# Loading wq in two pieces and wo's row blocks 26 to 29 in one, in a cached attention decode kernel with a gated feed-forward branch

## The chip, the cores and the metric

The kernel runs on one core of one Trainium2 chip. The core has a matrix engine (TensorE, PE in the profile, with PEld for its weight loads), a vector engine (VectorE, DVE), an activation engine (ScalarE, ACT), GpSimd (POOL) and SyncE (SP), which here only issues transfers. Sixteen DMA engines move data between HBM and the on-chip memory of 128 partitions. The metric is the device time in microseconds (us) of one execution. What the profiler sees of an execution, from its first to its last instruction, is called the span.

## What is computed

One token passes through an attention block with a long cache and through a feed-forward block, and a scalar gate mixes the two:

```python
g = sigmoid((x * gate_w).sum(-1))             # x: 512 numbers
q = (x @ wq).reshape(32 heads, 128)            # wq: 512 x 4096
scores = q . k_cache * 128 ** -0.5             # 8 groups of 4 heads, 32768 positions
o = softmax(scores) . v_cache                  # k_cache, v_cache: 8 x 32768 x 128
a = o.reshape(4096) @ wo                       # wo: 4096 x 512
b = (silu(x @ w_gate) * (x @ w_up)) @ w_down   # 512 x 1792, 512 x 1792, 1792 x 512
out = g * a + (1 - g) * b
```

All inputs are bf16. The two caches are 67 MB each; wq and wo are 4.2 MB each and the three feed-forward matrices 1.8 MB each. Everything is read once, 148 MB in all.

## The kernel before

**Memory.** One tensor, `page`, holds three pages of 64 KB in each of the 128 partitions. A K or V group (8.4 MB) fills one page. K groups go by turns into pages 0 and 1, V groups into page 2. Until V0 comes, page 2 holds wq (32 KB per partition) and the gate and up matrices behind it. After the last K group, page 0 takes `w_down` and wo.

**Transfers.** SP issues all loads on one queue, in an order that is written out by hand (lines 349 to 387): wq, x and `gate_w` (one row of 1 KB each), gate, up, K0 in two halves, K1, and then by turns a K group and a V group, each behind a wait for the page to be free. K1 needs no wait. V0 waits until TensorE has finished with gate and up (`sem_pe_h`), since they share page 2 with wq. K2 waits for the 32 transposes of K0 (`sem_tr`), V1 for the last matmul on V0 (`sem_v_done`). The last V group comes in four pieces, and then wo comes in the pieces of `WO_CUTS` (line 59), each with a semaphore of its own. wo is seen as 32 row blocks: every partition holds 32 rows of 512 numbers, and a block is one such row on all partitions, 1 KB each.

**The head.** TensorE transposes x and `gate_w` (L383), VectorE writes the columns into a zero-padded tile and multiplies them for the gate, and TensorE waits for wq (`sem_q`, line 393) before the q projection and then the gate and up projections (L400, 64 matmuls). VectorE turns q into blocks (`qblk`, L637) and computes the feed-forward activations.

**The groups.** For every K group VectorE transposes 32 units of the page into two slots (L707), and TensorE multiplies each with q (L445) into the scores. VectorE takes the maximum (L716), GpSimd reduces it over partitions (L308), ScalarE takes the exponentials (L567) and rearranges them (L580), and TensorE multiplies them with the V group (L472). TensorE goes through the groups in a loop in which V of one group comes ahead of the scores of the next.

**The tail.** TensorE multiplies the attention output with wo. Row blocks 0 to 19 are taken by `emit_wide` as rows of 512 columns (L517). The blocks behind them go through `emit_wo` and `emit_rows` (lines 236 to 258, L239), four matmuls of 128 columns per block, which wait for the semaphore of each piece. The pieces from index `KL` = 4 on are taken at lines 764 and 765, outside of the main block, so the branch out of that block (L267) lies in front of them. Then VectorE copies the row to bf16 (L768), and SP and ScalarE's queue store half of it each (L262).

Of the kernel before, what the change touches and what calls it, by code (L numbers as in the profile page):

```python
# [14 lines left out]
def bass_gated_mix__gqa_block_cached__swiglu_ffn__decode_kernel(  # L15
# [23 lines left out]
    KC = D // 128  # L39
# [16 lines left out]
    assert S % 128 == 0 and NT == 256 and G == 8 and RB * NS * 4 == 4096  # L56
    assert KC * H * DH + 2 * KC * F <= PAGE and (FC + WOJ) * NOUT <= PAGE

    WO_CUTS = [0, 16, 20, 24, 26, 28, 30, 32]
    KW = 2  # L60
    KL = 4
    WIDE = WO_CUTS[KW]
    RQ = 4
# [13 lines left out]
    assert RQ * HPG <= 32 and RQ * DH == 512 and FC % 2 == 0  # L77
    assert WO_CUTS[-1] == WOJ and FC % 2 == 0

# [7 lines left out]
    with ExitStack() as es:  # L87
        def S_(name):
            return es.enter_context(nc.semaphore(name))

        sem_q = S_("s_q")
# [9 lines left out]
        sem_ld_wd = S_("s_ld_wd")  # L101
        sem_wo = [S_(f"s_wo{i}") for i in range(len(WO_CUTS) - 1)]
        sem_tr = S_("s_tr")
# [99 lines left out]
        wq_v = page[:, w0 : w0 + KC * H * DH].rearrange("p (c n) -> p c n", c=KC)  # L203
# [29 lines left out]
        def rows(p, a, b):  # L233
            return page[:, p * PAGE + a * DH : p * PAGE + b * DH]

        def emit_rows(pe, lhs, rhs, last):
            for oc in range(OC):
                e = oc % RPS
                ins = pe.matmul(  # L239
                    ps_c[32 * oc : 32 * oc + (1 if e else SW), 0:128],  # L240
                    lhs(e),
                    rhs[:, oc * 128 : (oc + 1) * 128],
                    start=False,
                    stop=last,
                    skip_group_check=True,
                )
            return ins

        def emit_wo(pe, k):
            pe.wait_ge(sem_wo[k], 16)  # L250
            for j in range(WO_CUTS[k], WO_CUTS[k + 1]):
                ins = emit_rows(
# [14 lines left out]
        with nc.Block("main") as block:  # L267
# [49 lines left out]
            @block.sync  # L317
            def _(sp):
                def cache(src, j, p, a=0, b=NT):
                    return sp.dma_start(  # L320
                        rows(p, a, b),
                        src[0, j, :, :].rearrange("(p r) d -> p r d", r=NT)[:, a:b, :].rearrange(
                            "p r d -> p (r d)"
                        ),
                    )

                def load_k(j):
                    if j >= K_PAGES:
                        sp.wait_ge(sem_tr, UNITS * (j - K_PAGES + 2))
                    p = j % K_PAGES  # L330
                    late = {0: sem_k0, G - 1: sem_k7}.get(j)
                    if late is None:
                        cache(A_k_cache, j, p).then_inc(sem_k[p], 16)
                    else:
                        cache(A_k_cache, j, p, 0, NT // KH).then_inc(sem_k[p], 16)
                        cache(A_k_cache, j, p, NT // KH, NT).then_inc(late, 16)

                def load_v(j):
                    if j:
                        sp.wait_ge(sem_v_done, VTURN * (j + 1))  # L340
                    else:
                        sp.wait_ge(sem_pe_h, KC)
                    if j < G - 2:
                        cache(A_v_cache, j, V_PAGE).then_inc(sem_v, 16)
                    else:
                        cache(A_v_cache, j, V_PAGE, 0, V6_CUT).then_inc(sem_v, 16)
                        cache(A_v_cache, j, V_PAGE, V6_CUT, NT).then_inc(sem_v6, 16)

                sp.dma_start(wq_v, A_wq.rearrange("(p c) n -> p c n", c=KC)).then_inc(sem_q, 16)
                sp.dma_start(x2[0:1, :], A_x[0, :, :]).then_inc(sem_ld_x, 16)  # L350
                sp.dma_start(x2[1:2, :], gate_w.unsqueeze(0)).then_inc(sem_ld_x, 16)
                for w, (src, sem) in enumerate(((B_w_gate, sem_fg), (B_w_up, sem_fu))):
                    sp.dma_start(
                        wgu[:, w, :, :], src.rearrange("(p c) f -> p c f", c=KC)
                    ).then_inc(sem, 16)
                load_k(0)
                for j in range(G - 1):
                    load_k(j + 1)
                    load_v(j)
                sp.wait_ge(sem_tr, UNITS * G)  # L360
                sp.dma_start(wd_v, B_w_down.rearrange("(p j) n -> p j n", j=FC)).then_inc(
                    sem_ld_wd, 16
                )
                def load_wo(k):
                    a, b = WO_CUTS[k], WO_CUTS[k + 1]
                    src = A_wo.rearrange("(p j) n -> p j n", j=WOJ)
                    sp.dma_start(wo_v[:, a:b, :], src[:, a:b, :]).then_inc(sem_wo[k], 16)  # L367

                for k, sem in enumerate(sem_v7):
                    a, b = V7_CUTS[k], V7_CUTS[k + 1]  # L370
                    sp.wait_ge(sem_v_done, VTURN * (G - 1) + b // (RQ * VB))
                    cache(A_v_cache, G - 1, V_PAGE, a, b).then_inc(sem, 16)
                for k in range(len(sem_wo)):
                    load_wo(k)

            @block.tensor
            def _(pe):
                def emit_q():
                    pe.wait_ge(sem_eye, 1)
                    pe.wait_ge(sem_ld_x, 32)  # L380
                    x2v = x2.rearrange("o (p c) -> o c p", c=KC)
                    for c in range(KC):
                        ins = pe.matmul(  # L383
                            ps_m[:, M_X0 + 2 * c : M_X0 + 2 * c + 2],
                            x2v[:, c, :],
                            eye2[:, :],
                            start=True,
                            stop=True,
                        )
                    ins.then_inc(sem_pe_x, 1)  # L390
                    pe.wait_ge(sem_dve_prod, 1)
                    pe.wait_ge(sem_xz, 2)
                    pe.wait_ge(sem_q, 16)
                    pe.wait_ge(sem_psw, 1)

                    def strips(c, base, n, width, at, ps):
                        x = [pe.compute_val(c * XW + (96 - 32 * s)) for s in range(NSTRIP)]
                        w = [pe.compute_val(c * n + (base + at(i))) for i in range(2 * NSTRIP)]
                        for i in range(2 * NSTRIP):
                            ins = pe.matmul(  # L400
                                ps_sc[:, ps(i) * 512 : ps(i) * 512 + width],
                                slot[:, bass.ds(x[i % NSTRIP], 128)],
                                page[:, bass.ds(w[i], width)],
                                start=False,
                                stop=False,
                                skip_group_check=True,
                            )
                        return ins

                    with pe.Fori(0, KC, 1) as c:  # L410
                        strips(
                            c, w0, H * DH, 512, lambda i: (2 * (i % 4) + i // 4) * 512, lambda i: i // 4
                        ).then_inc(sem_pe_q, 1)
                    pe.wait_ge(sem_fg, 16)
                    pe.wait_ge(sem_fu, 16)
                    with pe.Fori(0, KC, 1) as c:
                        strips(
                            c, w1, F, FS, lambda i: (i // 4) * KC * F + (i % 4) * FS, lambda i: 2 + i // 4
                        ).then_inc(sem_pe_h, 1)
                    pe.wait_ge(sem_const, 4)  # L420
                    pe.wait_ge(sem_dve_qT, 1)
                    qc0 = q_blk.rearrange("p (n l) -> p n l", l=QP)[:, :, 0]
                    for s in range(NSTRIP):
                        ins = pe.matmul(
                            ps_m[:, M_P0 + s * 32 : M_P0 + (s + 1) * 32],
                            spread[:, s, :],
                            qc0,
                            start=True,
                            stop=True,
                        )  # L430
                    ins.then_inc(sem_pe_qp, 1)
# [75 lines left out]
                def emit_wide():  # L507
# [5 lines left out]
                    for k in range(KW):  # L513
                        pe.wait_ge(sem_wo[k], 16)
                        for j in range(WO_CUTS[k], WO_CUTS[k + 1]):
                            c = j % NSTRIP
# [13 lines left out]
                    for k in range(KW + 1, KL):  # L530
                        emit_wo(pe, k)

                emit_q()
                with hinted(pe, "groups", 1, G + 4) as (p, arm):
                    with pe.If(p < G + 3):
# [227 lines left out]
        pe, dve = nc.tensor, nc.vector  # L763
# [37 lines left out]
```

## Time and profile before

| what | us |
|---|---|
| median of three runs | 349.87 (349.70 to 349.89) |
| the profiled execution | 349.6 |
| its span | 348.2 |
| VectorE busy | 191.2 |
| TensorE matmuls busy | 182.1 |
| ScalarE busy | 92.8 |
| wq, from its issue to its landing | 12.4 |
| wo's first piece (2 MB), from issue to landing | 24.9 |
| wo's four pieces of 256 KB, median from issue to landing | 26.8 |

The page gives the busy time of each engine over the span; the forty slices show when it lies. Time from issue to landing counts the waiting behind earlier transfers of the same queue, so that a late landing need not be a slow transfer. The DMA view of a stretch gives the packets that began in it and the time they took as a share of sixteen engines; from the two the mean time of one packet can be worked out. A packet carries the row of one partition. In a short stretch the share can be over 100%, because a packet counts where it begins.

### The profile page before, as it was taken

The numbers are of one execution on the slowest core, as the hardware profiler recorded it, in microseconds if no ns is written. First come the engines' busy times: TensorE is split into PE (matmuls) and PEld (weight loads), VectorE is DVE, ScalarE is ACT, GpSimd is POOL, SyncE is SP. The second block draws the span as 40 slices with busy tenths as digits, with TensorE's granted clock in tenths as the row PEclk, the third lists the DMA queues.
The fourth block names the chain that finished last, engine by engine and source line by source line (L and its number), as shares of the span: only waits on it lengthen the run. The fifth ranks groups of instructions, "written<-read, shape, count | busy, mean of one in ns | idle before, by whom it ended". The sixth has DMA issues, their size and how long they took to land.

```text
span 348.2 us, 7729 instructions
## 1 busy us (share of the span) xinstructions
PE 182.1 (52%) x2755; PEld 111.1 (32%) x2755; DVE 191.2 (55%) x311; ACT 92.8 (27%) x220; POOL 8.3 (2%) x29
## 2 busy tenths in 40 slices
PE   0393553555425570565435560556445485667555
PEld 0141442443124420443124420443134334432112
DVE  4024996996059911995069802994079829940001
ACT  1002001901730039002630057003630066037000
POOL 4000000000000000000000000000000000000000
PEclk9999555555855556555855576555655576559856
DMA  8999989989899898998989989899898999999996
GB/s 324 419 459 425 482 384 459 474 369 482 376 467 474 369 482 369 474 474 369 482 369 474 474 369 482 369 474 474 369 482 369 440 448 429 422 413 430 429 427 261
DMA packets 4766, 148.14 MB, mean 425 GB/s; under 512 B 538, under 2 KB 540, under 8 KB 1308
## 3 DMA queue, kind: packets, MB, share of 16 engines
q1 hardware_dynamic: 4760, 148.12, 98.9%
q8 instruction: 1, 0.02, 0.0%
q14 instruction: 1, 0.01, 0.0%
q10 hardware_dynamic: 4, 0.00, 0.0%
HBM read 148.11 MB, written 0.00 MB: 425 GB/s over the span
## 4 chain that ended last, share of the span: by engine, by line
DMA 49%; PE 21%; DVE 18%; issue 9%; SPq 2%; DVEq 1%; ACT 0%
DMA page<-in_A_k_cache_dram 39%; DVE slot L707 17%; PE ps_sc L445 9%; DMA page<-in_A_wo_dram 7%; PE ps_o L472 7%; PE ps_sc L400 4%; DMA E<-in_gate_w_dram 3%; SPq L367 2%; DVE qblk L637 0%; SPq L320 0%; DVE E L654 0%; DVE oT L695 0%; DVEq L703 0%; DVE E L663 0%; PE ps_o L486 0%
## 5 line engine op out<-in xcount | busy, mean ns | idle before, releaser
L707 DVE STREAM_TRANSPOSE slot<-page 128x512 f32<-128x512 f32 x256 | 167.0, 690 | 92.9 <-DMA page<-in_A_k_cache_dram 80.9
L445 PE MATMUL ps_sc<-qcur,slot 128*128 128x16 bf16 x2048 | 103.8, 179 | 119.7 <-DVE slot L707 106.4
L445 PEld LDWEIGHTS ps_sc<-qcur,slot 128*128 128x128 bf16 x2048 | 81.2, 107 | 143.3 <-issue 142.2
L472 PE MATMUL ps_o<-page,ET 128*16 128x512 bf16 x512 | 47.5, 546 | 19.7 <-issue 15.2
L580 ACT ACTIVATE ET<-E 32x256 bf16<-32x256 bf16 x128 | 52.8, 412 | 1.4
L562 ACT ACTIVATE nbias<-gmax 128x4 f32<-128x4 f32 x8 | 1.6, 206 | 179.1 <-POOL gmax L308 179.1
L472 PEld LDWEIGHTS ps_o<-page,ET 128*16 128x16 bf16 x512 | 16.0, 117 | 47.6 <-issue 37.9
L567 ACT ACTIVATE E<-ps_sc,nbias 128x256 bf16 x32 | 21.8, 851 | 1.8 <-ACT nbias L562 1.8
L400 PE MATMUL ps_sc<-page,slot 128*128 x64 | 14.8, 391 | 1.0 <-DVE prod_col L618 1.0
L716 DVE TENSOR_REDUCE pmax<-ps_sc 128x4 f32<-128x1024 f32 x8 | 9.8, 1225 | 4.7 <-PE ps_sc L445 4.7
L739 DVE TENSOR_REDUCE oT<-ps_o 128x4 f32<-128x64 f32 x1 | 0.2, 224 | 21.3 <-PE ps_o L486 21.3
L562 ACT ACT_TABLE_LOAD x8 | 10.3, 1283 | 0.1
L576 ACT ACTIVATE acc<-ps_o 128x512 f32<-128x512 f32 x8 | 4.8, 606 | 20.4 <-PE ps_o L472 20.4
L308 POOL PARTITION_ALL_REDUCE gmax<-pmax x8 | 3.0, 371 | 292.1 <-DVE pmax L716 292.1
L400 PEld LDWEIGHTS ps_sc<-page,slot 128*128 x64 | 6.6, 103 | 8.9 <-issue 3.8
L567 ACT ACTIVATION_READ_ACCUMULATOR E<-ps_sc,nbias x32 | 9.3, 290 | 0.0
L486 PE MATMUL ps_o<-ident_f,acc 128*128 128x128 f32 x32 | 5.7, 305 | 5.6 <-ACT acc L576 4.9
L383 PE MATMUL ps_m<-eye,E 2*128 2x2 bf16 x4 | 0.3, 166 | 13.2 <-DMA E<-in_gate_w_dram 13.2
L486 PEld LDWEIGHTS ps_o<-ident_f,acc 128*128 128x128 f32 x32 | 3.6, 150 | 10.0 <-ACT acc L576 8.4
L498 PE MATMUL ps_w<-page,vec 128*1 x14 | 5.3, 376 | 2.2 <-issue 0.8
L627 DVE CAST E<-ps_sc 128x1024 bf16<-128x1024 f32 x1 | 1.2, 1225 | 8.8 <-PE ps_sc L400 8.8
L614 DVE CAST xT<-ps_m 128x4 bf16<-128x4 f32 x1 | 0.2, 163 | 8.3 <-PE ps_m L383 8.3
(63 smaller groups left out, 34.6 us busy)
## 6 DMA issues: line engine op xcount, KB each, us to landing
page<-in_A_k_cache_dram SPq DMA_DIRECT2D x4, 4096.0 KB, 36.9
page<-in_A_v_cache_dram SPq DMA_DIRECT2D x2, 4096.0 KB, 22.4
page<-in_A_wq_dram SPq DMA_DIRECT2D x1, 4096.0 KB, 12.4
page<-in_A_v_cache_dram SPq DMA_DIRECT2D x2, 2048.0 KB, 14.0
page<-in_A_v_cache_dram SPq DMA_DIRECT2D x1, 3072.0 KB, 14.3
page<-in_A_wo_dram SPq DMA_DIRECT2D x1, 2048.0 KB, 24.9
page<-in_B_w_gate_dram SPq DMA_DIRECT2D x1, 1792.0 KB, 15.6
page<-in_B_w_up_dram SPq DMA_DIRECT2D x1, 1792.0 KB, 19.5
```

The source lines that it names most:

```text
L367: sp.dma_start(wo_v[:, a:b, :], src[:, a:b, :]).then_inc(sem_wo[k], 16)
L400: ins = pe.matmul(ps_sc[:, ps(i) * 512 : ps(i) * 512 + width], slot[:, bass.ds(x[i % NSTRIP], 128)], page[:, bass.ds(w[i], width)], start= ...
L445: ins = pe.matmul(ps_sc[:, bass.ds(c0 + u * (SLOTS * RPU * NS) + (s * RPU + r) * NS, NS),], sv[:, s, r, e // 2, e % 2, :], qcur[:, e, :], ...
L472: ins = pe.matmul(ps_o[32 * c : 32 * c + VW, :], ET[:, k * VW : (k + 1) * VW], rows(V_PAGE, n, n + RQ), start=(k < NSTRIP), stop=(k >= NT ...
L486: ins = pe.transpose(ps_o[:, q * 128 : (q + 1) * 128], acc[:, q * 128 : (q + 1) * 128], ident_f[:, :],)
L498: pe.matmul(ps_w[0:1, :], vec[:, bass.ds(n, 1)], page[:, bass.ds(n * NOUT + o0, NOUT)], start=False, stop=False, skip_group_check=True,)
L562: act.activation(nbias[:, :], gmax[:, :], ACT.Copy, scale=-SCALE).then_inc(sem_nbias, 1)
L567: act.activation(ev[:, h, :, :], scv[:, h, :, :], ACT.Exp, bias=nbias[:, h : h + 1], scale=SCALE, accum_out=esum[:, bass.ds(j * HPG + h, 1 ...
L576: act.activation(acc[:, :], ps_o[:, :], ACT.Copy).then_inc(sem_acc, 1)
L580: ins = act.activation(etv[QP * i : QP * (i + 1), :, g, :], E[QP * g : QP * (g + 1), i * w : (i + 1) * w].rearrange("p (f m) -> p f m", f=KH),
L707: dve.transpose(slot_f[:, s * (SLOT // 2) : (s + 1) * (SLOT // 2)].rearrange("p (x g b) -> p g x b", g=NQ, b=QP), kp[:, f, :, tu * UW : (t ...
L716: dve.tensor_reduce(pmax[:, :], ps_sc[:, p * RB * NS : (p + 1) * RB * NS].rearrange("p (x h) -> p h x", h=HPG), AX.X, ALU.max,).then_inc(s ...
```

## The change

The load of wq becomes two loads, in the same place of the queue: first partitions 0 to 15 (16 rows of 32 KB), then partitions 16 to 127 (112 such rows). Both increment the same semaphore, and TensorE's wait goes from 16 to 32. In `WO_CUTS` the cut at 28 is taken out: row blocks 26 to 29 come in one load of 512 KB instead of two of 256 KB, with one semaphore and one wait less. The last piece, blocks 30 and 31, is as before. The bytes, their addresses and the matmuls stay, and so does the order of instructions on every engine but SP. SP issues as many loads as before.

```diff
-    WO_CUTS = [0, 16, 20, 24, 26, 28, 30, 32]
+    WO_CUTS = [0, 16, 20, 24, 26, 30, 32]
...
-                sp.dma_start(wq_v, A_wq.rearrange("(p c) n -> p c n", c=KC)).then_inc(sem_q, 16)
+                wq_src = A_wq.rearrange("(p c) n -> p c n", c=KC)
+                for a, b in ((0, 16), (16, 128)):
+                    sp.dma_start(wq_v[a:b, :, :], wq_src[a:b, :, :]).then_inc(sem_q, 16)
...
-                    pe.wait_ge(sem_q, 16)
+                    pe.wait_ge(sem_q, 32)
```

## The prediction

> **What bounds the kernel now.** I read the page's head, its forty slices and its queues first, then the busy time by stage, then the chain that ended last, then the DMA view of short stretches.
>
> The page of the kernel before, head, slices, queue and idle groups:
>
> ```profile
> span 348.2 us, 7729 instructions
> ...
> DVE  4024996996059911995069802994079829940001
> ...
> DMA  8999989989899898998989989899898999999996
> GB/s 324 419 459 425 482 384 459 474 369 482 376 467 474 369 482 369 474 474 369 482 369 474 474 369 482 369 474 474 369 482 369 440 448 429 422 413 430 429 427 261
> ...
> q1 hardware_dynamic: 4760, 148.12, 98.9%
> ...
> HBM read 148.11 MB, written 0.00 MB: 425 GB/s over the span
> ...
> L707 DVE STREAM_TRANSPOSE slot<-page 128x512 f32<-128x512 f32 x256 | 167.0, 690 | 92.9 <-DMA page<-in_A_k_cache_dram 80.9
> ```
>
> See the packets of q1: they fill 98.9% of sixteen DMA engines' span. VectorE, the busiest compute engine, works 55% of it, and most of its idle time ends with a K load. So the end is set by when the transfers are through, plus a short head and tail.
>
> The stage view (length, then busy time of PE, PEld, DVE, ACT, POOL, then granted clock, DMA share and GB/s) says whether there is a hole anywhere:
>
> ```profile
> 0.00:1.70 1.70, 0.00 (x0) 0.00 (x0) 0.43 (x1) 0.90 (x1) 0.85 (x7) 1.00 0.00 0
> ...
> 14.00:30.00 16.00, 14.98 (x68) 6.88 (x68) 2.97 (x5) 0.92 (x3) 0.40 (x1) 1.00 1.02 440
> 30.00:56.00 26.00, 12.22 (x240) 9.55 (x240) 23.60 (x42) 1.10 (x1) 0.00 (x0) 0.58 1.03 444
> 56.00:100.00 44.00, 19.79 (x340) 13.19 (x340) 24.75 (x40) 22.34 (x54) 0.75 (x2) 0.58 0.99 429
> 100.00:300.00 200.00, 105.94 (x1780) 69.62 (x1780) 124.77 (x198) 56.60 (x135) 1.85 (x5) 0.57 1.00 433
> 300.00:340.00 40.00, 24.51 (x247) 9.72 (x247) 9.64 (x19) 10.59 (x27) 1.33 (x3) 0.67 1.00 427
> ```
>
> The share is 0.99 to 1.03 from 14 to 340 us, whatever the row size (14 KB, 32 KB or 64 KB). There is no hole in which a late transfer could catch up: microseconds that the sixteen DMA engines lose at the start stay lost to the end.
>
> The chain that ended last (start, us, what), its head and tail:
>
> ```profile
> 0.74 0.38 SPq L349
> 1.17 0.32 SPq L350
> 1.55 11.48 DMA E<-in_gate_w_dram
> ...
> 14.42 13.07 PE ps_sc L400 x56
> ...
> 321.66 24.48 DMA page<-in_A_wo_dram
> 346.14 0.04 issue
> 346.19 0.33 PE ps_c L239 x4
> ```
>
> At the head TensorE waits for `gate_w`, which queues behind wq. At the tail the last piece of wo lands at 346.14, and 0.33 of matmul, the copy and the store follow.
>
> The DMA view of 5 to 9 us, where only wq's 32 KB packets (one per partition) move:
>
> ```profile
> DMA packets 58, 1.90 MB, mean 475 GB/s; under 512 B 0, under 2 KB 0, under 8 KB 0
> ...
> q1 hardware_dynamic: 58, 1.90, 110.0%
> ```
>
> One such packet takes 1.100 x 16 engines x 4 us / 58 = 1.214 us, and wq's 128 are 8 per engine: 8 x 1.214 = 9.7 us.
>
> **The change, part by part.** The profiled execution took 349.6 us, of which the span is 348.2 and 1.4 lies around it; the median of the three runs, 349.87, is 0.27 more. The sum is made on 349.6, and 0.27 is added at the end.
>
> *One more issue on SP, ahead of everything.* x, `gate_w`, gate, up and K0 are issued about 0.4 us later (wq's issue took 0.38). The queue holds 9.7 us of wq by then, so the transfers cover this; SP next has to act at 29 us, when V0 follows TensorE. Without that cover it would cost 0.4. Taken: 0.
>
> *The start.* The first sixteen packets are slow: the DMA view from 1.7 to 2.6 us shows 16 packets at 209.1%, so 2.091 x 0.9 = 1.88 us each. A load of one row per engine may be set up sooner. Bounds: 0, and -0.67 (1.88 - 1.21). Should the DMA engines instead wait between the two loads, the second issue costs at most its 0.4. Taken: 0, since nothing shows what the first 1.88 us are spent on.
>
> *Sixteen rows on sixteen neighbouring partitions.* 512 KB in one packet per engine, if sixteen engines share it. In the trace sixteen engines are always spread over 128 partitions, and then each packet takes 1.214 us. What sixteen neighbours can take in is not shown. Ends: every engine has its own path into them (x1, loss 0), or all sixteen share one (x16, 18.2 us lost). For lack of a nearer row I take the middle factor, four engines to a path: 4 x 1.214 = 4.86, a loss of 3.64 us on every DMA engine. [...]
>
> *112 rows in sevens.* Per engine 7 x 1.214 = 8.5 us alone. Before, each engine has eight rows that no other's path disturbs (full rate in every stage); 112 rows dealt in sevens cannot keep that division, so an engine's rows cross into another's. Ends: no row meets another engine (0), or each of the seven does (x2, 8.5 lost; if sixteen neighbours were taken at a time, more). I take two of seven for the worst engine: 2 x 1.214 = 2.43. The worst counts, because every later load is split evenly over engines that are never idle, and the last piece of wo waits for the last engine.
>
> *The wait for wq* (32 in place of 16) is passed when both parts have landed. Behind it on TensorE stand the q projection (13.07 us in the chain), the first K group and all later groups; VectorE's `qblk` and transposes, and V0's issue on SP, wait for these. If wq lands 6 us later they move 6 us, from 29.3 to 35 for V0's issue and from 56.7 to 63 for K2's. The 33.0 MB issued ahead of K2 (wq, gate, up, K0, K1, V0) keep the queue full to about 1.7 + 76 = 78 us at 433 GB/s, and move by the same 6 us. So this costs nothing beyond the transfer itself; only if the chain came 78 - 57 = 21 us later than the transfers would SP leave the queue empty.
>
> *wo's row blocks 26 to 29 in one load.* From 343.1 to 345 us 360 packets of 2 KB, with their completions, fill 105.7%: 1.057 x 16 x 1.9 / 360 = 0.089 us each. From 340.6 to 342.3, 170 of 4 KB fill 102.5%: 0.164 each. Two loads are 16 x 0.089 = 1.43 us per engine, one is 8 x 0.164 = 1.31. Saved: 0.12, directly in front of the last landing. One issue and 128 packets fewer also ease SP, whose last wo issues took 3.24 and 5.43 us; the last ended at 327, 19 us before landing, so that is worth 0. TensorE had to wait for row 27's block until its branch out of the main block was through: its sixteen matmuls of blocks 26 to 29 all start at 345.69, so waiting for both at once delays none of them unless the merged load lands later than that.
>
> Sum: +3.64 + 2.43 - 0.12 = +5.95; 349.6 + 5.95 + 0.27 = 355.8 us.
>
> **The rivals.**
>
> *The landing place is not what limits.* Then each packet takes 1.214 us wherever it goes, and only the small terms are left. For it: the trace shows no DMA engine slowed by another. Against it: no sixteen engines there ever work on sixteen neighbours. Price: -0.12 and half of the start's bound, -0.33, so 349.4: no change that counts.
>
> *The same, and the first row per engine starts at once.* The whole 0.67 of the start comes back on the slowest engine, which the spread of the first packets (all sixteen begin in 0.9 us) could have carried to the end: 349.87 - 0.67 - 0.12 = 349.1. This is the faster side; it decides if more than 0.58 of the 0.67 is regained (0.70 less 0.12) and the landing is not shared.
>
> [...]
>
> *The 112 rows are dealt one by one.* Sixteen neighbours are then written at every step and all eight steps pay 3.64: 8 x 3.64 = 29 us, 379.
>
> **How the numbers follow.** About 0.2% is what a measurement of this kernel can tell from no change: 0.70 us, so 349.17 to 350.57. Shared landing, as forecast: 0.66. Dealt one by one: 0.04. Unlimited landing or owner rule, with little of the start regained: 0.16. The same with most of it regained: 0.14. So slower 0.70, same 0.16, faster 0.14.
>
> The forecast's own range: the first load at x3 and no loss in the second, 2.4 - 0.12, 352.2; the first at x4 and four of seven rows shared, 3.64 + 4.86 - 0.12, 358.3. For 8 in 10 it must reach into the other cases: down to 349.0 (the whole start, and 0.1 beneath it) and up to 359.0.
>
> **What would show it.** If right: the first slice of the page falls from 324 GB/s to about 200; in the DMA view the first sixteen packets take near 5 us instead of 1.88; the q projection begins near 20 us instead of 14.42; the share after 30 us is again 0.99 to 1.03, and K2, K4, K6 and the last wo piece land some 6 us later, each by the same amount. The merged load shows as one wo issue of 512 KB, with no idle time on TensorE ahead of blocks 26 to 29 beyond the branch's 0.71. [...]

## The result and the profile after

| | before | changed |
|---|---|---|
| median, us (six runs each) | 349.74 (349.51 to 349.89) | 358.95 (358.54 to 359.19) |
| profiled execution, us | 349.6 | 358.97 |
| its span, us | 348.2 | 357.5 |

The changed kernel is slower: 1.0263 times the time before, 95% interval 1.0250 to 1.0276. That is 9.2 us on the medians and 9.3 us on the two spans.

The page of the changed kernel, head, slices and queue:

```profile
span 357.5 us, 7729 instructions
...
DVE  4002599699407970499119940797049927950002
...
DMA  9899999989999998998998999899899899999996
GB/s 176 235 336 434 455 418 469 455 374 462 462 403 425 469 447 374 469 455 367 469 455 374 462 462 447 381 469 455 367 469 455 367 455 418 422 424 447 414 433 247
...
q1 hardware_dynamic: 4632, 148.12, 98.9%
```

The bytes are the same 148.12 MB, and packets still take up 98.9% of the sixteen DMA engines' span. The DMA slices look as full as before. Only the GB/s line says where the time went: the first three slices move 176, 235 and 336 GB/s, against 324, 419 and 459. From 1.7 to 14 us the DMA share is 1.04 at 221 GB/s; before it is 1.00 at 408 GB/s there. The busy share alone does not show this loss.

By stage (length, busy time of PE, PEld, DVE, ACT and POOL, granted clock, DMA share, GB/s):

```profile
1.70:14.00 12.30, 0.00 (x0) 0.00 (x0) 3.22 (x4) 0.38 (x1) 3.16 (x12) 1.00 1.04 221
14.00:21.50 7.50, 0.00 (x0) 0.00 (x0) 0.00 (x0) 0.00 (x0) 0.00 (x0) 1.00 0.96 227
21.50:30.00 8.50, 6.86 (x27) 2.92 (x28) 0.51 (x4) 0.20 (x1) 0.40 (x1) 1.00 1.08 453
30.00:56.00 26.00, 15.39 (x175) 9.39 (x173) 17.68 (x31) 1.83 (x2) 0.00 (x0) 0.71 0.99 428
56.00:100.00 44.00, 24.71 (x448) 17.24 (x448) 33.15 (x52) 14.02 (x36) 0.75 (x2) 0.51 1.01 438
100.00:300.00 200.00, 99.28 (x1680) 65.24 (x1672) 116.01 (x183) 61.93 (x148) 1.85 (x5) 0.60 1.00 433
```

Until 21.5 us the rate is 221 to 227 GB/s, and from there on it is what it was before: 433 GB/s from 100 to 300 us in both kernels. The whole loss is made while wq moves, and nothing of it comes back.

TensorE's waits up to 40 us, and SP's queue (start, us, issue):

```profile
PE ps_m L385 <- DMA E<-in_gate_w_dram: 21.9, 1, 21.9
PE ps_sc L402 <- DMA page<-in_A_wq_dram: 1.2, 1, 1.2
```

```profile
0.74 0.85 SPq L351 DMA_DIRECT2D page<-in_A_wq_dram  x2
1.64 0.32 SPq L352 DMA_DIRECT2D E<-in_A_x_dram  x1
...
38.68 0.33 SPq L320 DMA_DIRECT2D page<-in_A_v_cache_dram  x1
66.10 0.33 SPq L320 DMA_DIRECT2D page<-in_A_k_cache_dram  x1
```

`gate_w`, which queues behind wq, releases TensorE at 21.9 us instead of 13.2. V0 is issued at 38.68 instead of 29.25 and K2 at 66.10 instead of 56.70. Both are 9.4 us late, like the transfers themselves, and the DMA share behind the head stays at 0.99 to 1.01, so the queue does not run empty. VectorE's wait for K pages stays at 81.0 us (80.9 before).

### The profile page after: what moved, and what is told of

It is laid out like the page before. It is cut to its first block, busy times and chain, and to the rows that moved or that the text cites. A ratio compares the mean times of both kernels' runs of the same rounds, so it can differ in the third digit from the quotient of the medians.

```text
span 357.5 us, 7729 instructions
## 1 busy us (share of the span) xinstructions
PE 180.0 (50%) x2755; PEld 110.9 (31%) x2755; DVE 191.2 (53%) x311; ACT 92.8 (26%) x220; POOL 8.3 (2%) x29
## 3 DMA queue, kind: packets, MB, share of 16 engines
q1 hardware_dynamic: 4632, 148.12, 98.9%
## 5 line engine op out<-in xcount | busy, mean ns | idle before, releaser
L474 PE MATMUL ps_o<-page,ET 128*16 128x512 bf16 x512 | 45.0, 523 | 20.1 <-issue 15.2
L385 PE MATMUL ps_m<-eye,E 2*128 2x2 bf16 x4 | 0.3, 166 | 21.9 <-DMA E<-in_gate_w_dram 21.9
L385 PEld LDWEIGHTS ps_m<-eye,E 2*128 2x128 bf16 x4 | 0.2, 110 | 21.9 <-issue 21.9
```

Of the source, the lines that this page charges most:

```text
L474: ins = pe.matmul(ps_o[32 * c : 32 * c + VW, :], ET[:, k * VW : (k + 1) * VW], rows(V_PAGE, n, n + RQ), start=(k < NSTRIP), stop=(k >= NT ...
```

## The experiments

All were built from the kernel before. Unless it says otherwise, wo is loaded as before. The diffs show the lines that make the loads; TensorE's wait goes up by 16 for every further load. The references are its medians beside the runs, 349.73 to 349.79 us.

### Which of the two edits

The split of wq alone:

```diff
+                for a, b in ((0, 16), (16, 128)):
+                    sp.dma_start(wq_v[a:b, :, :], wq_src[a:b, :, :]).then_inc(sem_q, 16)
```

> wq in the two loads of the change (partitions 0 to 15, 16 to 127), wo's pieces as before. Landing theory (the place where rows land is shared, and the two loads of wq lose the 9.2 us): 359.0, that is the changed kernel's 358.95 plus the 0.1 that the merged wo load saves. Rival, the merged wo load costs at the tail: clearly below 358.9, by what the merge costs.

Measured: 359.07 us (358.64 to 359.14), ratio 1.0263 (1.0248 to 1.0279). The whole loss comes with the split of wq.

wo's merged load alone:

```diff
-    WO_CUTS = [0, 16, 20, 24, 26, 28, 30, 32]
+    WO_CUTS = [0, 16, 20, 24, 26, 30, 32]
```

> wq in one load as before, wo's blocks 26 to 29 in one load. By the prediction's packets (sixteen of 2 KB at 0.089 us against eight of 4 KB at 0.164): 0.12 us less than before, 349.6. Rival, the tail now waits: in the changed kernel all 24 last matmuls start together and take 0.66 us, before the last 8 took 0.33; then 0.2 more than before, 349.9 to 350.0.

Measured: 349.61 us against 349.79, ratio 0.9996 (0.9987 to 1.0005). The sign fits the 0.12 us that was predicted, but the interval holds 1. The rival's 349.9 to 350.0 is not what came out, though the interval's upper end, 349.96, touches it. Its premise does not hold either: in the changed kernel only sixteen of the last 24 matmuls start together, at 355.19 us. The last eight start at 355.52, just behind the landing of the last piece at 355.48.

### Two loads, or loads of few partitions

wq in two loads again, but both over all 128 partitions, with wo merged as in the changed kernel:

```diff
+                for a, b in ((0, 1), (1, KC)):
+                    sp.dma_start(wq_v[:, a:b, :], wq_src[:, a:b, :]).then_inc(sem_q, 16)
```

> wq in two loads again, but cut along the row: first 8 KB of every partition, then the other 24 KB of every partition; wo's blocks merged. Landing theory: every load covers all 128 partitions with eight rows per engine, so nothing is shared and nothing lost: 349.6 to 349.9 (eight rows of 8 and of 24 KB take 0.313 and 0.915 us against 1.214, which is 0.11 more, and the merge saves 0.12); if a small first load shortens the start, down to 349.0. Rival, two loads of wq behind one semaphore cost as such: near 359.

Measured: 349.41 us (349.14 to 349.73), ratio 0.9990 (0.9981 to 0.9999). Two loads of wq behind one semaphore cost nothing as such. This is the one version whose interval leaves out 1 on the faster side, and only just: 0.4 us, of which the merged wo load may be a part (0.18 alone, not told from none). From 1.7 us on its first load, 128 rows of 8 KB, goes through like this:

```profile
DMA packets 124, 1.02 MB, mean 350 GB/s; under 512 B 0, under 2 KB 0, under 8 KB 0
...
q1 hardware_dynamic: 124, 1.02, 99.4%
```

These 124 packets take 0.994 x 16 x 2.9 / 124 = 0.372 us each, the cold start included; the 8 KB packets of the V7 pieces, late in the kernel before, take 0.997 x 16 x 1 / 51 = 0.313 (51 packets at 99.7% from 333.2 to 334.2 us). By these means the start costs each DMA engine an estimated 8 x 0.06 = 0.5 us here, against the 0.67 that the first packets of before lost. That a small first load shortens the start is argued from this, not shown by itself.

### The landing place or the source

Eight loads of sixteen rows, in four ways: the partitions that they land on are neighbours or eight apart, and the rows of wq that they read are neighbours or eight apart.

```diff
+                for a in range(8):
+                    sp.dma_start(wq_v[16 * a : 16 * a + 16, :, :], wq_src[16 * a : 16 * a + 16, :, :]).then_inc(sem_q, 16)
```

with `[a::8, :, :]` on one side or on both in the other three.

> wq in eight loads of sixteen neighbouring partitions each, rows as they lie in memory; wo as before. Landing theory with four engines to a path: every row takes 4 x 1.214 us, 3.64 lost in each of eight loads, 349.7 + 29.1 = 379. If the first load of the changed kernel is the measure (its last engine done near 5.4 us, where the first rows of before were through at 3.6 to 4.3): 1.1 to 1.8 lost per load, 359 to 364. If the rate goes with the number of partitions (sixteen of 128, eight times the time): 349.7 + 68 = 418.

> wq in eight loads of sixteen rows again, but each takes partitions eight apart (a, a + 8, ... a + 120), with their own rows of wq; wo as before. Landing theory: neighbours share, so that partitions eight apart lose clearly less than sixteen neighbours. Source theory (sixteen engines that read neighbouring rows of wq disturb each other): also less than sixteen neighbours, since the rows read are 256 KB apart; this run alone does not tell the two apart, the next two do. [...]

> Eight loads that land on sixteen neighbouring partitions each, but read rows of wq that are eight apart. wq's rows land on other partitions than theirs, so q comes from the wrong rows of wq; bytes and work stay the same. Landing theory: as the loads of sixteen neighbours with neighbouring rows, 379 if four share a path. [...]

> Eight loads that land on sixteen partitions eight apart, but read sixteen neighbouring rows of wq. Again wq's rows land on other partitions than theirs and q comes from the wrong rows; bytes and work stay. [...] Source theory: as the loads of sixteen neighbours, near 379.

| median, us (two runs each) | source rows neighbours | source rows eight apart |
|---|---|---|
| land on sixteen neighbours | 375.96 | 375.69 |
| land eight apart | 359.79 | 360.07 |

The ratios are 1.075 (1.073 to 1.077) and 1.0743 (1.0712 to 1.0775) in the first line, 1.0289 (1.0259 to 1.0318) and 1.0297 (1.0267 to 1.0326) in the second. Where the rows come from makes no difference that these runs tell; where they land makes 16 us. The source theory falls. For sixteen neighbours the 379 of the forecast's factor four comes nearest; 359 to 364 and 418 fall.

The DMA view inside wq, on sixteen neighbours (9 to 32 us) with neighbouring source rows:

```profile
DMA packets 160, 2.62 MB, mean 114 GB/s; under 512 B 80, under 2 KB 80, under 8 KB 80
...
q1 hardware_dynamic: 160, 2.62, 101.2%
```

and eight apart on both sides (6 to 18 us):

```profile
DMA packets 160, 2.62 MB, mean 218 GB/s; under 512 B 80, under 2 KB 80, under 8 KB 80
...
q1 hardware_dynamic: 160, 2.62, 105.1%
```

Of the 160 packets 80 are rows; the other 80 are under 512 B and come sixteen to a load (with seven loads more, the page counts 650 of them, 538 before). A row takes 1.012 x 16 x 23 / 80 = 4.66 us on sixteen neighbours, and 1.051 x 16 x 12 / 80 = 2.52 us eight apart, against 1.214 in a load of 128: 3.8 and 2.1 times.

### How far the sharing reaches

```diff
+                for a in range(0, 128, 32):
+                    sp.dma_start(wq_v[a : a + 32, :, :], wq_src[a : a + 32, :, :]).then_inc(sem_q, 16)
```

> wq in four loads of 32 neighbouring partitions (two rows per engine); wo as before. Landing theory, neighbours share and the loss falls as a load covers more: between the loads of sixteen neighbours and one load. If the rate goes with the number of partitions, 32 of 128 take four times 1.214 us: 349.7 + 29 = 379. [...]

Measured: 359.75 us, ratio 1.0288 (1.0258 to 1.0317). The loss of 10.0 us lies between the 26.2 of the loads of sixteen neighbours and the none of one load, as the landing theory has it; the 379 does not come out.

The same with steps of 64:

> wq in two loads of 64 neighbouring partitions (four rows per engine); wo as before. If the rate goes with the number of partitions that a load covers, 64 take twice 1.214 us per row: +9.7, 359.4. If what counted were that the landing is shared only among close neighbours, 64 should lose less than the four loads of 32, which lost 10.0: 354 to 357. If halves share as quarters do (two engines to a path in both): +10.0, 359.7, the same as the four loads of 32.

Measured: 360.23 us, ratio 1.0301 (1.0281 to 1.0322). The 354 to 357 of close neighbours falls. The DMA view from 6 to 18 us, of the loads of 32 and of those of 64:

```profile
DMA packets 128, 2.62 MB, mean 218 GB/s; under 512 B 48, under 2 KB 48, under 8 KB 48
...
q1 hardware_dynamic: 128, 2.62, 105.5%
```

```profile
DMA packets 96, 2.62 MB, mean 218 GB/s; under 512 B 16, under 2 KB 16, under 8 KB 16
...
q1 hardware_dynamic: 96, 2.62, 105.7%
```

Both are 80 rows, 2.53 and 2.54 us each. A load of 64 partitions is as slow per row as one of 32, so the rate does not go with the number of partitions. 114, 218 and 218 GB/s for 16, 32 and 64 neighbours, against the 433 of the K and V groups on all 128, are near a quarter, a half and a half. What makes these steps is not shown: the trace has packets, and not what they share where they land.

### What the 112 rows cost

```diff
+                for a, b in ((0, 112), (112, 128)):
```

> wq in the change's two sizes, but in the other order and place: partitions 0 to 111 first, then 112 to 127; wo as before. If the sixteen rows alone make the loss, it is that of one of the eight loads of sixteen, 26.2 / 8 = 3.3: 353.0. If the 112 rows in sevens cost by themselves, as the rest of the changed kernel's 9.2 says (5.9 or so), the sum comes out again whatever the order: 357 to 360. If the 112 rows are harmless at the start and only suffered from the engines that the sixteen rows had put out of step: 353 to 354.

Measured: 358.78 us, ratio 1.0260 (1.0239 to 1.0280): the loss of the changed kernel in the other order. The DMA view from 4 to 10 us, where only rows of the 112 move and no load of sixteen has gone before:

```profile
DMA packets 37, 1.21 MB, mean 202 GB/s; under 512 B 0, under 2 KB 0, under 8 KB 0
...
q1 hardware_dynamic: 37, 1.21, 82.1%
```

That is 0.821 x 16 x 6 / 37 = 2.13 us per row. From 10 to 14 us it is 1.216 x 16 x 4 / 40 = 1.95; both means are far above the 1.214 of a full load. The 112 rows are slow by themselves; the sixteen need not put the DMA engines out of step first, and the forecasts of 353 to 354 fall. That it is at the landing, as with sixteen neighbours, is inferred: no run here gives 112 rows other places or other sources.

### Another matrix, early and late

The gate matrix (third in the queue, rows of 14 KB) in the two loads, and in the other kernel `w_down`, which is issued at 286 us:

```diff
+                    for a, b in ((0, 16), (16, 128)) if w == 0 else ((0, 128),):
...
+                for a, b in ((0, 16), (16, 128)):
+                    sp.dma_start(wd_v[a:b, :, :], wd_src[a:b, :, :]).then_inc(sem_ld_wd, 16)
```

> wq and wo as before; instead the gate matrix, third in the queue, comes in two loads, partitions 0 to 15 and 16 to 127, with rows of 14 KB. Landing theory, loss in proportion to the bytes: 9.3 x 14336 / 32768 = 4.07 us, 353.8. Rival, a fixed cost of a load with few partitions: near 359. Rival, the loss belongs to the cold start of the queue: near 349.8.

> wq and wo as before; instead w_down, which is issued at 286 us behind the V6 load, comes in two loads, partitions 0 to 15 and 16 to 127, rows of 14 KB. Landing theory without a hole in the queue anywhere: the same loss as for the gate matrix at the start, +4.07, 353.8. Rival, late in the kernel the engines or the tail have some reserve that takes it up: clearly less, 350 to 352.

Measured: 353.74 us for gate, ratio 1.0113 (1.0096 to 1.0130), and 353.55 us for `w_down`, ratio 1.0117 (1.0100 to 1.0134). That is 4.0 and 3.8 us, where the bytes gave 4.07; a fixed cost of the load, a loss of the cold start alone and a reserve late in the kernel all fall. The loss goes with the bytes that are loaded in this shape (9.2 us for 4.2 MB, 4.0 and 3.8 for 1.8 MB), and it is nearly the same at the head of the queue and near its end. The DMA share of before, 0.99 to 1.03 from 14 to 340 us, left no hole to take it up.

## Why the prediction came out, and where it was off

**What bounds the kernel**: right. The microseconds that the DMA engines lost on wq and behind it, 8.4 and 0.6 each (below), came out at the end as 9.2; the two loads of gate, at the start, cost 4.0 and those of `w_down`, late, 3.8.

**The one more issue on SP**: right. Two issues of wq take 0.85 us, x is issued at 1.64 instead of 1.17, and every later landing follows the transfers.

**The start**: nothing was taken for it. The changed kernel can't show a gain there, as its first packets are slower. The DMA view from 1.7 to 2.6 us, before and changed:

```profile
DMA packets 16, 0.52 MB, mean 583 GB/s; under 512 B 0, under 2 KB 0, under 8 KB 0
...
q1 hardware_dynamic: 16, 0.52, 209.1%
```

```profile
DMA packets 16, 0.52 MB, mean 583 GB/s; under 512 B 0, under 2 KB 0, under 8 KB 0
...
q1 hardware_dynamic: 16, 0.52, 407.9%
```

The changed kernel's first rows take 4.079 x 0.9 = 3.67 us each, where near 5 were forecast.

**Sixteen rows on sixteen neighbours, 3.64 us**: right in kind. In size it is nearly right for a load with others ahead of it: eight such loads lost 375.96 - 349.79 = 26.2 us, 3.3 each, and a row's 3.8 times is near the factor of four. No run shows a path or how many DMA engines share one; in its place they show 4.66 us per row at 114 GB/s. In the changed kernel, though, these sixteen rows are the first of all, and the first rows took 1.88 us before as well: 3.67 - 1.88 = 1.8 us lost, half of the term. The forecast reckoned 4.86 against the 1.214 of later rows, on top of a slow start that it took for unchanged. The factor was a middle between ends far apart when it was chosen, and no row of the trace before could have given it.

**112 rows in sevens, 2.43 us**: this is the term that was mis-sized most. Two of seven rows were taken to meet another engine's. No run shows which rows meet; the trace shows every row slowed, the shortest of the 112 taking 1.70 us. That is nearer to the other end that was named (each of the seven, 8.5 lost). The DMA view of the changed kernel from 5 to 20 us:

```profile
DMA packets 124, 3.60 MB, mean 240 GB/s; under 512 B 14, under 2 KB 14, under 8 KB 14
...
q1 hardware_dynamic: 124, 3.60, 98.8%
```

110 rows at 0.988 x 16 x 15 / 110 = 2.16 us, 0.94 more than the 1.214 of a full load; seven of them lose 6.6 us. With the 1.8 of the sixteen rows that is 8.4, against 9.2 measured. The trace gives the same sum another way: wq's 128 packets take 301.6 us in all instead of 166.5, which is 8.4 more on each of sixteen engines. Another 0.6 lies in the gate matrix right behind: its 128 packets take 78.6 us in all instead of 68.5, the first of them beginning while rows of wq still move.

**The sum and the range**: the sum was +5.95. One term was 1.8 too large and the other 4.2 too small, so the errors in part made up for each other. Four of seven rows shared, the upper case of the forecast's own range, gave 358.3; the range was then widened to 359.0, and 358.95 lies inside by 0.05. The direction was foreseen, and that rows on sixteen neighbours take longer; that the range held the time was luck.

**wo's merged load, 0.12 less**: not contradicted and not shown; alone it gives 0.18 less, with an interval that holds no change. TensorE waits for its branch in front of blocks 26 to 29 as long as before (0.71 us), and the last landing, at 355.48 us, still decides when the last matmuls start.

**The wait for wq**: right. The q projection begins at 23.40 us instead of 14.42, where near 20 was forecast. V0 and K2 are issued 9.4 us later instead of 6, the later K groups 8.0 to 9.7, and the last piece of wo lands 9.3 us later (346.14 before).

**The rivals**: an unlimited landing, with or without a faster start, falls by the table of landing and source. The owner rule, which shares its chances, stands for no loss as well and falls by the 9.2 us. Dealing the 112 rows one by one was put at 29 us, and the load lost 6.6. Which rows of the 112 slow which stays open: the trace has the time of a packet, but not its partition.

## What to carry to other kernels

Try loads over all 128 partitions first, and where a load has to be cut, try the cut along the row. In this kernel wq, with rows of 32 KB, lost 9.2 us in two loads cut at partition 16, 10.5 cut at 64, and nothing cut along the row; with rows of 14 KB the cut at 16 lost 4.0 and 3.8. The DMA share before was 0.99 to 1.03 from 14 to 340 us, and the loss went to the end whether it was made early (wq, gate) or late (`w_down`), at 2.1 to 2.2 us per MB. Read the GB/s line beside the DMA share, for the share stayed full where the rows took longer: 1.04 at 221 GB/s from 1.7 to 14 us, 1.00 at 408 before.

## What the runs showed of the hardware that was not expected

The 112 rows of 128 came almost as badly off, at 2.16 us per row (2.13 and 1.95 in the two stretches on partitions 0 to 111), as a load of half the partitions at 2.54. One might have taken 112 of 128 for seven eighths of the way to a full load. And 64 neighbouring partitions were no faster per row than 32 (2.54 and 2.53 us), and no faster than sixteen that stand eight apart (2.52).
